# A convolution and a two-layer feed-forward block in one kernel: how the first layer's three passes are ordered and combined

## The chip, the core and the metric

The kernel runs on one core of a Trainium2 chip. Each time is the device time of one execution in microseconds; three runs of the kernel before are given and their median is the figure that counts. The profile comes from one profiled execution. TensorE (PE; its weight loads are listed as PEld), VectorE (DVE), ScalarE (ACT), GpSimd (POOL) and SyncE (SP, which here only starts DMA transfers) each have an instruction queue of their own and wait for one another by semaphores.

## The reference

The input `x` has 8 sequences of 4096 tokens with 192 channels. A causal convolution with seven taps, whose weights are a softmax over the taps of each head, gives 32,768 tokens of 192 channels. Then two dense layers with a gate between them:

```python
w = softmax(weight)                     # per head, over the 7 taps
y = causal_conv(x, w)                   # (32768, 192)
h = y @ w_in                            # (32768, 2048)
g = h * np.clip(h + 3.0, 0.0, 6.0) / 6.0
out = g @ w_out                         # (32768, 192), float32
```

## The kernel before, in words

**Blocks.** The tokens are worked off in 32 blocks of 1024. Block 0 is run by a start section of its own, while the weights are being loaded and converted; blocks 1 to 31 are each one call of `first_layer` followed by one call of `second_layer`. A block's 1024 tokens stand as two groups of 512: partitions 0 to 63 of the tile `y` hold the lower 512 tokens, partitions 64 to 127 the upper 512, and the 192 channels are three thirds of 64. A 64-row matmul uses half of TensorE's array, so a matmul on the lower half (`k` = 0) and one on the upper half (`k` = 1) can run side by side; they write two different PSUM banks. `y_other` holds the same parts with the two halves exchanged (each exchange is two DMA transfers on SyncE, lines 266 and 267), so that each chunk of `w_in` meets each token group.

**First layer.** `h = y @ w_in` is done per unit: a unit is one chunk of 128 hidden columns, from one half of the hidden columns on the lower array half and from the other on the upper one, for 512 tokens each. There are 16 units per block, 8 with `y_own` and 8 with `y_other`. A unit owns a slot, that is two PSUM banks out of eight; there are four slots, handed out in turn from `free_slots`. To keep nearly full float32 precision with TensorE's shorter number format (`fp32r` in the profile), each operand is split into a high part and a rest, and each unit makes three passes of six matmuls (three thirds, two array halves), line 516. In the kernel before, the three operands are HIGH, LOW and MIX, and the sum is built in two steps: after the passes HIGH and LOW the slot's two banks are multiplied in place by 4097 on ScalarE (line 528; for the last unit of a block ScalarE and VectorE take one bank each, lines 531 and 532), and the pass MIX is added on top. To give ScalarE the time, `first_layer` works two units ahead: `begin(n)` issues a unit's passes HIGH and LOW and the scaling, `end(n)` the pass MIX, and TensorE's order is begin 0, begin 1, end 0, begin 2, end 1, and so on; near the end begin 15 is issued ahead of end 13. `end(n)` then computes the gate: ScalarE's relu from PSUM into the tile `g` (`relu`, line 302) and VectorE's product with `h` from PSUM (`gate`, line 306), after which the slot may be used again.

At the first unit of each block one more matmul is issued first (line 508): lower half, one third, 256 columns, with the same operands as the full matmul that later overwrites its output. Within a pair, the upper half (`k` = 1) is issued first.

**Second layer.** `out = g @ w_out` is done with full float32 matmuls, 32 output columns each, four side by side (line 623), by a scheme that saves multiplications with sums of quarter matrices (`g_sums`, `small_sums`: lines 412, 456, 586 on VectorE and GpSimd). Its order is written out by hand as events with a due time: four streams of matmuls, and jobs `do(t, ...)` sorted in among them. The list `between` puts work for the next block there: `split_high` at 13, `split_rest` at 15, `swap_parts` at 18 (the parts of `y` and their exchange), and the load and first taps of the convolution for the block after next. The convolution's remaining taps (line 929, VectorE) are jobs in the first layer: one ahead of the units (`jobs[-1]`, together with what is left of the block before: two additions, their transposes and stores), and one each behind units 1, 5 and 9.

**The start.** `out_direct(0, ...)` is block 0's second layer (line 341). Between its matmuls `prepare` makes the parts of `w_in` (`w_parts`, in two halves of 1536 elements a partition: lines 474, 477, 485), convolves block 1, starts a load of `x` through GpSimd's queue and splits `y`; then `begin_block_two` makes sums of `w_out` and, on GpSimd, eight differences (line 595).

Each engine works through its instructions in the order in which the program issues them; nothing reorders them later.

Of the kernel before, what the change touches and what calls it, by code (L numbers as in the profile page):

```python
# [8 lines left out]
ALU = mybir.AluOpType  # L9
ACT = mybir.ActivationFunctionType  # L10
AX = mybir.AxisListType
F32 = mybir.dt.float32
# [5 lines left out]


CUT = 1.0 - 2.0**-13  # L20
EPS = 2.0**-12
HIGH, LOW, MIX = range(3)


@with_exitstack
def kernel(
# [8 lines left out]
    nc = tc.nc  # L35
    P = nc.NUM_PARTITIONS
# [6 lines left out]
    N = 512  # L43
    G = 2
    TB = G * N
    D2 = P // 2
    K3 = D // D2
# [7 lines left out]
    NP = NC // 2  # L55
# [32 lines left out]
    for base, dma in ((0, nc.scalar), (D2, nc.sync)):  # L88
        dma.dma_start(  # L89
            out=w_sb[base : base + D2],  # L90
            in_=weight.unsqueeze(1).to_broadcast([H, GJ, KC]),
# [126 lines left out]
    for n in range(AHEAD):  # L218
# [8 lines left out]
        out=e_sb[:], in0=w_sb[:], in1=mx[:].to_broadcast([P, KC]), op=ALU.subtract  # L227
# [4 lines left out]
    half = cst.tile([P, 1], F32, name="half")  # L232
# [4 lines left out]
    y = ys.tile([P, K3, N], F32, name="y")  # L237
# [27 lines left out]
    def swap(to, part):  # L265
        nc.sync.dma_start(out=to[D2:P], in_=part[0:D2])
        nc.sync.dma_start(out=to[0:D2], in_=part[D2:P])
# [10 lines left out]
    psum = ps.tile([P, 2 * 4, N], F32, name="psum")  # L278
# [22 lines left out]
    def relu(r6, h):  # L301
        nc.scalar.activation(r6, h, ACT.Relu, bias=half[:], scale=1.0 / 6.0)  # L302

    def gate(g_, h):

        nc.vector.scalar_tensor_tensor(  # L306
            out=g_, in0=g_, scalar=1.0, in1=h, op0=ALU.min, op1=ALU.mult
        )
# [93 lines left out]
    def g_sums(engine, which, slots, width):  # L402

        forms = {
            3: (S3, A11, A21, ALU.subtract),
            2: (S2, S1, A11, ALU.subtract), 4: (S3, A12, S2, ALU.subtract),
        }
        for n in which:
            o, a, b, op = forms[n]
            for p in slots[::width]:  # L410
                r = slice(p, p + width)
                engine.tensor_tensor(out=o[:, r], in0=a[:, r], in1=b[:, r], op=op)  # L412
# [42 lines left out]
    def add(out, x, y, op=ALU.add):  # L455
        nc.vector.tensor_tensor(out=out, in0=x, in1=y, op=op)  # L456
# [13 lines left out]
    def r32(ap):  # L470
        return ap.bitcast(F32R)

    def high_of(out, x, scale=1.0):
        nc.scalar.mul(r32(out), x, CUT * scale)

    def from_high(out, high, scale, x, op):
        nc.vector.scalar_tensor_tensor(
            out=r32(out), in0=high, scalar=scale, in1=x, op0=ALU.mult, op1=op
        )

    def w_parts(high, low, mix, w):
        high_of(high, w, EPS)
        from_high(mix, high, 4097.0, w, ALU.subtract)
        from_high(low, high, -4096.0, w, ALU.add)
        nc.scalar.mul(r32(mix), mix, -4096.0)

    free_slots = list(range(4))
    y_own, y_other, pools, s1 = [], [None], [], []

    def swap_parts():  # L490
        y_other[0] = pools[0].tile([P, 3, K3, N], F32, name="y_other", tag="other")
        for n in range(3):
            swap(y_other[0][:, n], y_own[n])


    def first_layer(i, jobs):

        slots = {}

        def both(n):  # L500
            return psum[:, 2 * slots[n] : 2 * slots[n] + 2]

        def mms(n, part, start=False, stop=False):
            group, c = divmod(n, NP)
            if n == 0 and start:

                r, half = slice(0, D2), slice(0, N // 2)
                nc.tensor.matmul(  # L508
                    out=psum[:, 2 * slots[n], half], lhsT=r32(w_in_parts[part][r, c, 0]),
                    rhs=r32(y_own[part][r, 0, half]), start=True, stop=False,  # L510
                    skip_group_check=True,
                )
            for s in range(K3):
                for k in (1, 0):
                    r = slice(k * D2, (k + 1) * D2)
                    nc.tensor.matmul(  # L516
                        out=psum[:, 2 * slots[n] + k], lhsT=r32(w_in_parts[part][r, c, s]),
                        rhs=r32(y_other[0][r, part, s] if group else y_own[part][r, s]),
                        start=start and s == 0, stop=stop and s == K3 - 1,
                        skip_group_check=True,  # L520
                    )

        def begin(n):
            slots[n] = free_slots.pop(0)
            mms(n, HIGH, start=True)
            mms(n, LOW)
            if n + 1 < count:
                nc.scalar.mul(both(n), both(n), 4097.0)  # L528
            else:
                lower, upper = (psum[:, 2 * slots[n] + k] for k in range(2))  # L530
                nc.scalar.mul(lower, lower, 4097.0)
                nc.vector.tensor_scalar(
                    out=upper, in0=upper, scalar1=4097.0, scalar2=None, op0=ALU.mult
                )

        def end(n):
            group, c = divmod(n, NP)
            mms(n, MIX, stop=True)
            to = g4[:, c, 1:3] if group else g4[:, c, 0::3]
            relu(to, both(n))  # L540
            gate(to, both(n))
            free_slots.append(slots[n])

        count = 2 * NP
        begin(0)
        begin(1)
        for job in jobs.get(-1, ()):
            job()
        for n in range(count):
            if n == count - 3:  # L550
                begin(n + 2)
            end(n)
            if n < count - 3:
                begin(n + 2)
            for job in jobs.get(n, ()):
                job()
            if n == 1:
                s1.append(ot.tile([P, NP, N], F32, name="s1", tag="shared")[:])
            if n < NP and n % 2:
                small_sums(s1[-1], A11, (1, 2, 3, 4), nc.gpsimd, every[n - 1 : n + 1])  # L560
            if n > NP and n % 2:
                pair = slice(n - NP - 1, n - NP + 1)
                g_sums(nc.gpsimd if n + 1 < count else nc.vector, (3,), range(NP)[pair], 2)
                if n + 3 < count:
                    nc.gpsimd.dma_start(out=S1[:, pair], in_=A22[:, pair], accum_op=ALU.add)
        for pair in (slice(NP - 2, NP), slice(NP - 4, NP - 2)):
            add(S1[:, pair], A21[:, pair], A22[:, pair])
# [7 lines left out]
    def small_sums(to, x, which, engine=nc.gpsimd, r=every):  # L575

        r = slice(r[0], r[-1] + 1)
        x11, x12, x21, x22 = four_parts(x[:, r])
        s1, s2, s3, s4 = four_parts(to[:, r])
        forms = {  # L580
            1: (s1, x21, x22, ALU.add), 2: (s2, s1, x11, ALU.subtract),
            3: (s3, x11, x21, ALU.subtract), 4: (s4, x12, s2, ALU.subtract),
        }
        for n in which:
            o, p, q, op = forms[n]
            engine.tensor_tensor(out=o, in0=p, in1=q, op=op)  # L586
# [222 lines left out]
    with tc.manual_schedule():  # L809
# [4 lines left out]
            out=c_sb[:], in0=e_sb[:], in1=sm[:].to_broadcast([P, KC]), op=ALU.mult  # L814
# [15 lines left out]
        for _ in range(3):  # L830

            nc.tensor.matmul(
                out=psum[:, b], lhsT=zeros[:, 0:P], rhs=zeros[:], start=True, stop=True
# [57 lines left out]
        slots = [0, 1, 3, 4, 6, 7, 9, 10, 12, 13]  # L891
        n = 3
# [30 lines left out]
        w_in_parts = [late.tile([P, NP, K3, P], F32, name=f"w_in{n}") for n in range(3)]  # L923
# [9 lines left out]
            return jobs  # L933

        def split_y():
            high, low, mix = y_own
            high_of(high[:], y[:])
            split_rest()

        def split_high():  # L940
            high_of(y_own[HIGH][:], y[:])

        def split_rest():
            high, low, mix = y_own
            nc.vector.tensor_tensor(out=r32(low[:]), in0=y[:], in1=high[:], op=ALU.subtract)
            from_high(mix[:], high[:], 1.0 + EPS, y[:], ALU.subtract)

        def prepare():
            for n in range(0, NP, 4):
                r = slice(n, n + 4)  # L950
                w_parts(*[w[:, r] for w in w_in_parts], w_in[:, r])
            for job in conv_jobs(1):
                job()
            first_in.close()
            later = ctx.enter_context(tc.tile_pool(name="later", bufs=1, reuse_waits="tile"))
            y_own.extend(later.tile([P, K3, N], F32, name=f"y{n}") for n in range(3))
            pools.append(ctx.enter_context(tc.tile_pool(name="oth", bufs=1, reuse_waits="tile")))
            x_tiles[2] = load_x(2, nc.gpsimd)
            split_y()
# [3 lines left out]
        def begin_block_two():  # L963
# [4 lines left out]
            for job in conv[:3]:  # L968
                job()

        out_direct(0, [prepare, lambda: None, begin_block_two])
        swap_parts()
        w_sums(((T3, B22, B12),))
# [53 lines left out]
```

## Time and profile before

| quantity | value |
|---|---|
| median of three runs | 2230.28 us |
| the three runs | 2229.96, 2230.28, 2230.80 us |
| profiled execution: span, first to last instruction | 2228.3 us |
| instructions | 50401 |
| granted TensorE clock, mean | 1.000 |
| busy PE / PEld | 2221.0 us (100%) / 1560.8 us (70%) |
| busy DVE / ACT / POOL | 1894.3 us (85%) / 1379.2 us (62%) / 823.6 us (37%) |
| matmuls of the first layer (L516), blocks 1 to 31 | 8928 |
| matmuls L508 | 31, 381 ns each |
| weight loads L516, mean | 184 ns |

For the profiled execution the records hold the span and no time of its own; the span lies 2.0 us under the median of the runs.

How to read it: "L516 PE MATMUL psum<-y,w_in 64*128 64x512" is a group of matmuls of line 516 that use 64 rows and 128 columns of the array and stream 512 columns; behind it stand the count, the busy time, the mean duration of one in ns, and the idle time of the engine just before them with what ended it. The durations of matmuls are modelled and overlap each other, so the rate of TensorE is read from starts, not from durations. The chain goes back from the last instruction, each time to what released it. TILE<-TILE names what is written and read: `psum<-psum` is an operation that works on PSUM in place. In a timeline's row stand the start, the time to the group's last end, the engine, the line, the operation and the count.

### The profile page before, as it was taken

What the parts mean: (1) busy time and instruction counts of PE and PEld (TensorE: products, weight loads), DVE (VectorE), ACT (ScalarE), POOL (GpSimd) and SP (SyncE); (2) the same over time, 40 slices, a digit from 0 to 9 for tenths busy, and PEclk for the clock granted to TensorE, in tenths of its full rate; (3) what the DMA queues carried; (4) which work ended last, traced back from release to release, by engine and by line L of the source; (5) the groups of instructions that cost most, each with busy time, mean ns of one, the idle gap of its engine ahead of it and who ended that gap; (6) DMA issues with size and microseconds to landing.
All of it is one profiled execution on the core that took longest, in us unless ns stands there. A gap on an engine that the chain in (4) does not pass through costs nothing.

```text
span 2228.3 us, 50401 instructions
## 1 busy us (share of the span) xinstructions
PE 2221.0 (100%) x21527; PEld 1560.8 (70%) x21527; DVE 1894.3 (85%) x1673; ACT 1379.2 (62%) x1678; POOL 823.6 (37%) x690
## 2 busy tenths in 40 slices
PE   9999999999999999999999999999999999999999
PEld 5477776677766777766777667786677776677766
DVE  8888888888888888888888888888888888888876
ACT  7457665576655676555766557665567655576654
POOL 2344432344422444223443234442244422344323
PEclk9999999999999999999999999999999999999999
DMA  6244224443244342344422443324434234442232
GB/s 157 58 98 84 49 58 91 85 83 63 53 82 91 77 80 46 71 91 84 84 48 58 91 87 81 67 49 82 91 78 82 47 67 91 84 84 52 55 77 34
DMA packets 253584, 166.58 MB, mean 75 GB/s; under 512 B 208016, under 2 KB 213136, under 8 KB 253360
## 3 DMA queue, kind: packets, MB, share of 16 engines
q1 hardware_dynamic: 234872, 129.46, 28.4%
q0 software_dynamic: 17248, 33.64, 8.7%
q8 instruction: 169, 2.77, 0.5%
q10 hardware_dynamic: 1240, 0.27, 0.1%
q14 instruction: 55, 0.45, 0.1%
HBM read 31.72 MB, written 25.17 MB: 26 GB/s over the span
## 4 chain that ended last, share of the span: by engine, by line
PE 99%; DMA 0%; DVE 0%; SPq 0%; ACT 0%; issue 0%; DVEq 0%; ACTq 0%
PE psum L623 49%; PE psum L516 46%; PE psum L296 2%; PE psum L341 2%; PE psum L508 0%; DMA x<-in_x_dram 0%; SPq L100 0%; SPq L133 0%; DVE top L175 0%; PE psum L824 0%; DVE y L255 0%; DVE results L456 0%; SPq L89 0%; ACT y L838 0%; ACT scale L186 0%
## 5 line engine op out<-in xcount | busy, mean ns | idle before, releaser
L623 PE MATMUL psum<-g,w_out 128*32 128x512 f32 (+1 forms) x6712 | 967.5, 552 | 0.0
L306 DVE SCALAR_TENSOR_TENSOR g<-g,psum 128x1024 f32<-128x1024 f32 (+1 forms) x528 | 618.3, 1186 | 203.6 <-ACT g L302 203.1
L586 POOL TENSOR_TENSOR s<-g 128x256 f32<-128x256 f32 x248 | 273.9, 1104 | 1244.4 <-DVE g L306 1244.4
L302 ACT ACTIVATE g<-psum,half 128x1024 f32<-128x1024 f32 (+1 forms) x528 | 564.8, 1086 | 4.9 <-PE psum L516 0.3
L623 PEld LDWEIGHTS psum<-g,w_out 128*32 128x32 f32 x6712 | 371.7, 110 | 246.0 <-issue 126.7
L516 PE MATMUL psum<-y,w_in 64*128 64x512 f32 x4464 | 524.9, 388 | 0.0
L516 PE MATMUL psum<-y_other,w_in 64*128 64x512 f32 x4464 | 516.1, 386 | 0.0
L528 ACT ACTIVATE psum<-psum 128x1024 f32<-128x1024 f32 x465 | 469.0, 1009 | 54.4 <-PE psum L516 52.1
L516 PEld LDWEIGHTS psum<-y,w_in 64*128 64x128 f32 x4464 | 435.4, 184 | 71.2 <-ACT psum L528 0.3
L516 PEld LDWEIGHTS psum<-y_other,w_in 64*128 64x128 f32 x4464 | 423.8, 184 | 82.1
L623 PE MATMUL psum<-s,w_out 128*32 128x512 f32 (+1 forms) x3272 | 465.5, 570 | 0.0
L929 DVE SCALAR_TENSOR_TENSOR y<-x,c_sb,y 128x1536 f32<-128x1536 f32 x186 | 335.3, 1803 | 2.6 <-ACT y L927 1.4
L412 POOL TENSOR_TENSOR s<-g 128x1024 f32<-128x1024 f32 x93 | 285.8, 3073 | 26.7 <-DVE g L306 26.5
L623 PE MATMUL psum<-g,w_s 128*32 128x256 f32 x1240 | 282.8, 379 | 0.0
L623 PEld LDWEIGHTS psum<-s,w_out 128*32 128x32 f32 x3272 | 154.3, 110 | 81.8 <-issue 49.4
L623 PEld LDWEIGHTS psum<-g,w_s 128*32 128x32 f32 x1240 | 136.4, 110 | 67.7
L412 DVE TENSOR_TENSOR s<-g 128x2048 f32<-128x2048 f32 (+1 forms) x93 | 181.3, 1977 | 1.1
L623 PE MATMUL psum<-s,w_s 128*32 128x256 f32 x744 | 170.7, 379 | 0.0
L586 DVE TENSOR_TENSOR g<-g 128x1024 f32<-128x1024 f32 x124 | 151.7, 1224 | 5.2
L412 DVE TENSOR_TENSOR g<-g 128x2048 f32<-128x2048 f32 x62 | 139.0, 2284 | 0.0
L620 ACT COPY psum<-psum 32x512 f32<-32x512 f32 x93 | 51.3, 551 | 135.4 <-PE psum L623 135.4
L456 DVE TENSOR_TENSOR results<-psum,results 32x256 f32<-32x256 f32 (+3 forms) x128 | 69.3, 541 | 50.9 <-issue 45.5
(93 smaller groups left out, 1316.6 us busy)
## 6 DMA issues: line engine op xcount, KB each, us to landing
y_other<-y SPq DMA_DIRECT2D x186, 384.0 KB, 5.1
g<-g POOLq DMA_DIRECT2D x62, 512.0 KB, 5.0
out_dram<-results SPq DMA_DIRECT2D x378, 64.0 KB, 2.0
x<-in_x_dram SPq DMA_DIRECT2D x53, 388.5 KB, 7.7
stage<-in_moe_w_in_dram SPq DMA_DIRECT2D x16, 192.0 KB, 4.8
stage<-in_moe_w_out_dram SPq DMA_DIRECT2D x8, 384.0 KB, 5.5
x<-in_x_dram SPq DMA_DIRECT2D x7, 384.0 KB, 8.3
x<-in_x_dram POOLq DMA_DIRECT2D x2, 388.5 KB, 5.3
```

What stands on the lines that cost most here:

```text
L296: nc.tensor.matmul(out=psum[:, b], lhsT=w[r], rhs=src, start=start, stop=stop, skip_group_check=onto,)
L302: nc.scalar.activation(r6, h, ACT.Relu, bias=half[:], scale=1.0 / 6.0)
L306: nc.vector.scalar_tensor_tensor(out=g_, in0=g_, scalar=1.0, in1=h, op0=ALU.min, op1=ALU.mult)
L341: lambda p=p: nc.tensor.matmul(out=bank[j * QS : (j + 1) * QS, tokens], lhsT=w_out[:, p, w, cols], rhs=x[:, p, tokens], start=(first and p ...
L412: engine.tensor_tensor(out=o[:, r], in0=a[:, r], in1=b[:, r], op=op)
L456: nc.vector.tensor_tensor(out=out, in0=x, in1=y, op=op)
L516: nc.tensor.matmul(out=psum[:, 2 * slots[n] + k], lhsT=r32(w_in_parts[part][r, c, s]), rhs=r32(y_other[0][r, part, s] if group else y_own[ ...
L528: nc.scalar.mul(both(n), both(n), 4097.0)
L586: engine.tensor_tensor(out=o, in0=p, in1=q, op=op)
L620: streams[3].append((t - 0.5, lambda: fn(*args, **kw)))
L623: nc.tensor.matmul(out=out, lhsT=w, rhs=x, start=start, stop=True, tile_position=(0, j * QS), skip_group_check=True,)
L929: jobs.append(lambda k=k: nc.vector.scalar_tensor_tensor(out=y[:], in0=x[:, :, k : k + N], scalar=c_sb[:, k : k + 1], in1=y[:], op0=ALU.mu ...
```

## The change

The three passes of a unit are now issued one after the other into the same slot, unit after unit, and add straight up: `w` HIGH with `y` HIGH, `w` LOW with `y` HIGH, `w` FULL with `y` LOW. The split is high = x times (1 - 2^-13) rounded to the short format, low = x - high. With `w = full`, this is w times low plus (high + low) times high. The in-place multiplication by 4097 goes, and with it `begin`, `end` and the two units of lead. `y` has two parts and not three, so two exchanges per block and not three. `w` keeps three parts: its LOW is now one subtraction on GpSimd, and FULL a copy on ScalarE. The extra matmul at the start of a block goes, and within a pair the lower half (`k` = 0) is issued first. The jobs of `jobs[-1]` are issued ahead of unit 0 (before: behind `begin(1)`, and thus ahead of unit 0's gate on VectorE too).

```diff
-HIGH, LOW, MIX = range(3)
+HIGH, LOW, FULL = range(3)
+PASSES = (HIGH, HIGH), (LOW, HIGH), (FULL, LOW)
...
-    def w_parts(high, low, mix, w):
-        high_of(high, w, EPS)
-        from_high(mix, high, 4097.0, w, ALU.subtract)
-        from_high(low, high, -4096.0, w, ALU.add)
-        nc.scalar.mul(r32(mix), mix, -4096.0)
+    def low_of(out, x, high, engine):
+        engine.tensor_tensor(out=r32(out), in0=x, in1=high, op=ALU.subtract)
+
+    def w_parts(high, low, full, w):
+        high_of(high, w)
+        nc.scalar.copy(out=r32(full), in_=w)
+        low_of(low, w, high, nc.gpsimd)
...
-        y_other[0] = pools[0].tile([P, 3, K3, N], F32, name="y_other", tag="other")
-        for n in range(3):
+        y_other[0] = pools[0].tile([P, 2, K3, N], F32, name="y_other", tag="other")
+        for n in range(2):
             swap(y_other[0][:, n], y_own[n])
...
-            if n == 0 and start:
-
-                r, half = slice(0, D2), slice(0, N // 2)
-                nc.tensor.matmul(
-                    out=psum[:, 2 * slots[n], half], lhsT=r32(w_in_parts[part][r, c, 0]),
-                    rhs=r32(y_own[part][r, 0, half]), start=True, stop=False,
-                    skip_group_check=True,
-                )
-            for s in range(K3):
-                for k in (1, 0):
...
-        def begin(n):
-            slots[n] = free_slots.pop(0)
-            mms(n, HIGH, start=True)
-            mms(n, LOW)
-            if n + 1 < count:
-                nc.scalar.mul(both(n), both(n), 4097.0)
...
-        def end(n):
-            group, c = divmod(n, NP)
-            mms(n, MIX, stop=True)
...
+        def unit(n):
             group, c = divmod(n, NP)
+            slot = free_slots.pop(0)
+            for m_, (wn, yn) in enumerate(PASSES):
+                for s in range(K3):
+                    for k in range(2):
+                        r = slice(k * D2, (k + 1) * D2)
+                        nc.tensor.matmul(
+                            out=psum[:, 2 * slot + k], lhsT=r32(w_in_parts[wn][r, c, s]),
+                            rhs=r32(y_other[0][r, yn, s] if group else y_own[yn][r, s]),
+                            start=m_ == s == 0, stop=m_ == 2 and s == K3 - 1,
+                            skip_group_check=True,
+                        )
+            both = psum[:, 2 * slot : 2 * slot + 2]
             to = g4[:, c, 1:3] if group else g4[:, c, 0::3]
-            relu(to, both(n))
-            gate(to, both(n))
-            free_slots.append(slots[n])
+            relu(to, both)
+            gate(to, both)
+            free_slots.append(slot)
...
         def split_rest():
-            high, low, mix = y_own
-            nc.vector.tensor_tensor(out=r32(low[:]), in0=y[:], in1=high[:], op=ALU.subtract)
-            from_high(mix[:], high[:], 1.0 + EPS, y[:], ALU.subtract)
+            low_of(y_own[LOW][:], y[:], y_own[HIGH][:], nc.vector)
```

More of the change, by code (lines that the diff above doesn't have):

```diff
@@ L20 @@
 CUT = 1.0 - 2.0**-13
-EPS = 2.0**-12
-HIGH, LOW, MIX = range(3)
+HIGH, LOW, FULL = range(3)
+PASSES = (HIGH, HIGH), (LOW, HIGH), (FULL, LOW)
 @with_exitstack
@@ L471, in r32, with high_of @@
         return ap.bitcast(F32R)
[L473 to L478, printed above, removed]
-        )
-    def w_parts(high, low, mix, w):
-        high_of(high, w, EPS)
-        from_high(mix, high, 4097.0, w, ALU.subtract)
-        from_high(low, high, -4096.0, w, ALU.add)
-        nc.scalar.mul(r32(mix), mix, -4096.0)
+    def high_of(out, x):
+        nc.scalar.mul(r32(out), x, CUT)
+    def low_of(out, x, high, engine):
[4 more added lines that the diff above has]
+        low_of(low, w, high, nc.gpsimd)
     free_slots = list(range(4))
@@ L490, in swap_parts @@
     def swap_parts():
-        y_other[0] = pools[0].tile([P, 3, K3, N], F32, name="y_other", tag="other")
-        for n in range(3):
+        y_other[0] = pools[0].tile([P, 2, K3, N], F32, name="y_other", tag="other")
+        for n in range(2):
             swap(y_other[0][:, n], y_own[n])
     def first_layer(i, jobs):
[L498 to L503, printed above, removed]
+        def unit(n):
@@ L504, in mms @@
             group, c = divmod(n, NP)
-            if n == 0 and start:
-                r, half = slice(0, D2), slice(0, N // 2)
-                nc.tensor.matmul(
-                    out=psum[:, 2 * slots[n], half], lhsT=r32(w_in_parts[part][r, c, 0]),
-                    rhs=r32(y_own[part][r, 0, half]), start=True, stop=False,
-                    skip_group_check=True,
-                )
-            for s in range(K3):
-                for k in (1, 0):
[L515 to L521, printed above, removed]
@@ L523, in begin @@
-        def begin(n):
-            slots[n] = free_slots.pop(0)
-            mms(n, HIGH, start=True)
-            mms(n, LOW)
-            if n + 1 < count:
[L528 to L534, printed above, removed]
@@ L539, in end @@
+            both = psum[:, 2 * slot : 2 * slot + 2]
             to = g4[:, c, 1:3] if group else g4[:, c, 0::3]
-            relu(to, both(n))
-            gate(to, both(n))
-            free_slots.append(slots[n])
+            relu(to, both)
+            gate(to, both)
+            free_slots.append(slot)
         count = 2 * NP
-        begin(0)
-        begin(1)
         for job in jobs.get(-1, ()):
@@ L549, in first_layer @@
         for n in range(count):
[L550 to L554, printed above, removed]
+            unit(n)
             for job in jobs.get(n, ()):
@@ L935, in split_y @@
         def split_y():
-            high, low, mix = y_own
-            high_of(high[:], y[:])
+            split_high()
             split_rest()
@@ L943, in split_rest @@
         def split_rest():
-            high, low, mix = y_own
-            nc.vector.tensor_tensor(out=r32(low[:]), in0=y[:], in1=high[:], op=ALU.subtract)
-            from_high(mix[:], high[:], 1.0 + EPS, y[:], ALU.subtract)
+            low_of(y_own[LOW][:], y[:], y_own[HIGH][:], nc.vector)
         def prepare():
@@ L955, in prepare @@
             later = ctx.enter_context(tc.tile_pool(name="later", bufs=1, reuse_waits="tile"))
-            y_own.extend(later.tile([P, K3, N], F32, name=f"y{n}") for n in range(3))
+            y_own.extend(later.tile([P, K3, N], F32, name=f"y{n}") for n in range(2))
             pools.append(ctx.enter_context(tc.tile_pool(name="oth", bufs=1, reuse_waits="tile")))
```

## The prediction

> **What bounds the kernel now.** I read the engine totals of the page first, then the chain that ended last, then one block of 1024 tokens (a repeating period) by stage, and last the starts of single matmuls.
>
> The page, sections 4 and 5:
>
> ```profile
> PE 99%; DMA 0%; DVE 0%; SPq 0%; ACT 0%; issue 0%; DVEq 0%; ACTq 0%
> L516 PE MATMUL psum<-y,w_in 64*128 64x512 f32 x4464 | 524.9, 388 | 0.0
> L528 ACT ACTIVATE psum<-psum 128x1024 f32<-128x1024 f32 x465 | 469.0, 1009 | 54.4 <-PE psum L516 52.1
> ```
>
> TensorE carries 99% of the chain, and its matmuls have 0.0 us of idle time. The scaled middle step (L528) is 469 us of ScalarE, and nothing of ScalarE is on the chain. So what counts is what the change does to TensorE's own succession. The chain of waits, cut to one block (start, us, what):
>
> ```profile
> 201.32 35.47 PE psum L623 x216
> 236.79 0.31 PE psum L508
> 237.10 8.00 PE psum L516 x69
> ```
>
> and engine busy time in that block's first layer (168.24 to 201.25) and second layer:
>
> ```profile
> 168.24:201.25 33.01, 33.01 (x290) 27.40 (x289) 25.85 (x23) 30.74 (x32) 21.95 (x19) 1.00 0.15 25
> 201.25:236.72 35.47, 35.47 (x386) 21.15 (x384) 32.76 (x28) 11.90 (x20) 3.59 (x2) 1.00 0.59 119
> ```
>
> Columns: stretch, us, then busy us (instructions) of PE, PEld, DVE, ACT, POOL, then clock, DMA share, GB/s. The reader is to see a period of 68.48 us, run 31 times, TensorE without a gap in either half at a clock of 1.00, and ScalarE at 30.74 of 33.01 us in the first half: nearly full, yet TensorE doesn't wait for it. In the waits of the weight loader, ScalarE's L528 stands with 0.3 us in two waits.
>
> How fast does TensorE step? A first-layer matmul has 64 rows; the lower (k=0) and the upper half (k=1) of the array work side by side, in pairs, 144 pairs a block. Matmul timelines, each of a narrow window (so the first start in it is read):
>
> ```profile
> 168.24 0.38 PE L508 MATMUL psum<-y,w_in 64*128 64x256 f32 x1
> 168.24 0.49 PE L516 MATMUL psum<-y,w_in 64*128 64x512 f32 x1
> 168.46 3.16 PE L516 MATMUL psum<-y,w_in 64*128 64x512 f32 x25
> 171.00 0.62 PE L516 MATMUL psum<-y,w_in 64*128 64x512 f32 x3
> 171.91 0.40 PE L516 MATMUL psum<-y,w_in 64*128 64x512 f32 x2
> 200.71 0.39 PE L516 MATMUL psum<-y_other,w_in 64*128 64x512 f32 x2
> ```
>
> L508 starts together with the upper half's first matmul, takes the lower half for 256 columns, and so puts the lower half half a step behind. From 168.46 to 171.00 lie 25 - 3 = 22 starts, 11 steps of 2.54/11 = **0.231 us**. Near 171.1 the two halves fall into step (two matmuls now start at 171.91 as one), and from pair 16 (171.91) to pair 143 (200.71) lie 127 steps of 28.80/127 = **0.2268 us**. The weight loader shows the same two states: in 168.45 to 171.05 it is busy 2.51 of 2.60 us (the two halves load in turn), in 171.65 to 200.90 it is 24.18 of 29.25 (both load at once).
>
> **The change, part by part.**
>
> *L508 goes, the order within a pair turns from (1, 0) to (0, 1).* Today pair 143 starts 200.71 - 168.24 = 32.47 us after the stage's first matmul. Without L508 I expect both halves to start at 168.24 in step. The first matmul shows its weight load: 0.49 us against the mean of 0.39, so the second pair comes 0.227 + 0.10 = 0.33 us later; the first-layer matmuls of the start, which have no such extra matmul, do just this (pairs at 17.12, 17.65 and 18.08, thus 0.53 and then 0.43). Then 141 steps of 0.2268 us = 31.98. Pair 143 starts after 32.31 us: **0.16 us less per block, 31 x 0.16 = 5.0 us**. It comes from two places: the lower half begins its first full matmul 0.22 us sooner, and 11 steps of 0.231 become 0.2268 (0.05 us); against them stands that the relock at 171.1 today costs the upper half, which ran ahead, and not the pair. Bounds of this unknown: were the halves to stay out of step all stage, 0.33 + 141 x 0.231 = 32.90, a loss of 0.43 us per block (13 us); were all of L508's piece in the chain to go, a gain of 0.31 us (9.6 us). I take 0.16, as 127 of 143 steps in every block already show the rate. The gap ahead of the stage (167.71 to 168.24) and the one behind it (200.94 to 201.25) stay.
>
> *Three passes in a row instead of 12 matmuls of two units ahead.* The number of L516 matmuls stays at 18 per unit, 8,928 in all, of the same shapes. In the order of TensorE a unit's sum is complete after 18(n+1) matmuls instead of 18n + 30; only the last three units (today at 276, 282, 288 of 288) change by more: 252, 270, 288. Every relu and gate (L302, L306) is thus ready as early as today or up to 24 matmuls sooner, so nothing in the second layer gets later.
>
> *The scaled middle step goes (L528, L531, L532).* Per block 15 x 1.01 + 0.58 = 15.7 us of ScalarE and 0.70 us of VectorE. All of it lies beside TensorE: worth nothing. What is late next is nothing on the path, as TensorE has no idle.
>
> *The waits that remain.* A unit's first matmul waits for the gate that frees its PSUM slot, four units before. Queued behind it is all of TensorE. Now the tile jobs of the block before (two adds, two transposes, one convolution tap) stand ahead of the first gate on VectorE, as they do today: they end at 171.63 + 1.77 = 173.4. Then gate 0 to 174.6, gate 1 to 175.8, a tap of 1.8 to 177.6, gate 2 to 178.8. Unit 4 begins at 168.24 + 0.33 + 35 x 0.2268 = 176.5, unit 6 at 180.6: the cover is 1.8 to 1.9 us (today unit 4 begins at about 175.9 and gate 0 ends at 174.9: 1.0). Units 1 to 3 take banks that the second layer leaves last; their waits come later than today (at matmul 18, 36, 54 instead of 12, 30, 48), and today they cost nothing. If one were late, it would cost at least one shown weight load, 0.10 us per block, 3.1 us.
>
> *The third operand goes.* Per block 1.76 us of VectorE (L477), and two of six y_other transfers of SyncE (384 KB, 5.1 us to landing), all during the second layer: hidden, worth nothing.
>
> *The weights' parts, once, during 58 to 100 us.* VectorE loses four operations of 1.91 us; ScalarE keeps four; GpSimd gets two subtractions of 128x1536. Its row for 128x1024 is 3.07 us, so an estimate of 4.6 us each. GpSimd's last join ends at 67.0, so they end near 76; the second pass that needs them begins at 100.5 (99.72 + 0.33 + two steps). Behind them on GpSimd stand the load of x for block 2, which today waits until 88.06 for VectorE, and the eight w_s differences from 89.37: unmoved. Cover 24 us; beyond it each us costs one.
>
> Sum: 2228.3 - 5.0 = 2223.3 us of span. The median of the three runs stands 2.0 us above the profiled span (2230.28 against 2228.3), and I carry that over: **2225.3 us**.
>
> **Where the Trainium skill speaks against this.** The row: 127 steps in step at 0.2268 us, weight loads hidden. The Trainium skill (TensorE: Matmul & The Clock Gate, Part 3, on what overlaps) says that a weight load runs beside matmuls in flight only where its row group is another one. By that rule it is the staggered start that hides loads, and removing L508 would expose one per pair. The rows speak against it: while in step, both halves load during their own matmuls.
>
> **Rivals.**
>
> 1. *The gain is eaten* (14%): one or two waits at the new unit borders end after TensorE arrives, 0.10 us each per block, one leaves 0.06 of the 0.16, two lose 0.04. Time 2228.4 or 2231.5. For it: each of the first three units waits now for ScalarE or VectorE; against it: those waits come 0.7 us later than today.
> 2. *Out of step* (9%), the slower side: without L508 the halves start 4 ns apart and drift into alternation as they do in 168.46 to 171.00, at 0.231 us. Price 0.43 us per block: 2243. It decides if the alternation holds past pair 40 or so: at 0.004 us a step, 40 steps eat the gain. Against it: after 171.1 nothing drifts.
> 3. *VectorE late for the slots* (3%): slower once VectorE runs over 1.8 us behind in a block; 1 us beyond costs 31 us: 2256. Against it: it idles before single gates already today.
> 4. *Loads exposed in step* (1%): 0.10 us for each of 142 steps, 31 times, 440 us: 2670. Against it are the 127 steps.
> 5. *All of the chain's piece goes* (6%): 0.31 us per block, 2220.7. For it: the chain shows it as a piece of its own; against it: the first matmul must then show its load instead.
> 6. *ScalarE paces the first layer* (1%), as its 98% in 171.65 to 200.90 would suggest: steps would fall toward the 0.215 of the second layer's half-width matmuls (L623 128x256, in the timeline two of them start 0.43 us after two others), 0.012 x 143 x 31 = 53 us, 2177. Against it: no idle on PE.
>
> **How the numbers follow.** Forecast 66%, with 0.13 to 0.19 us per block: 2224.4 to 2226.3. The runs of before spread by 0.8 us, so its own range is 2224.2 to 2226.6. Forecast and rival 1 hold 80%: the range is 2224.2 to 2231.5, and leaves out rivals 2 to 6. A measurement of this kernel can tell about 0.2% from no change, 4.5 us, that is 0.144 us per block; most of the forecast (54 of 66) lies beyond it. Faster: 54 + 6 + 1 = 61%. Same: 12 + 14 = 26%. Slower: 9 + 3 + 1 = 13%.
>
> **What would show it right or wrong.** After the change a block's period should be 68.33 us; the stage's two first matmuls should both last 0.49 and start together; the weight loader should stand near 83% from the stage's first microsecond; ScalarE should fall by 487 us to some 892, VectorE by 84 us to some 1810, with PE still 99% of the chain. It is wrong if the stage's early steps are 0.231 (rival 2), if a unit border shows a matmul of 0.49 us again (rival 1), or if PE's load waits name DVE or ACT in the first layer (rival 3).

## The result, and the profile after

| | before | after |
|---|---|---|
| median of 14 runs each | 2230.24 us | 2225.70 us |
| ratio, 95% interval | | 0.998 [0.9972, 0.9988] |
| profiled span | 2228.3 us | 2223.6 us |
| a block's period (first matmul of one first layer to that of the next, median of the blocks) | 68.487 us | 68.340 us |
| busy PEld / DVE / ACT / POOL | 1560.8 / 1894.3 / 1379.2 / 823.6 us | 1536.0 / 1810.3 / 938.1 / 819.8 us |
| moved by DMA | 166.58 MB | 142.10 MB |

The kernel is 4.5 us faster; 2225.3 us was forecast. The period accounts for the gain: 31 x (68.487 - 68.340) = 4.56 us. Lines after the change are numbered anew: the first layer's matmuls are L508 (before L516), the second layer's L593 (before L623), relu L308, gate L312.

The page of after, sections 4 and 5:

```profile
PE 99%; DMA 0%; DVE 0%; SPq 0%; ACT 0%; issue 0%; DVEq 0%; ACTq 0%
L308 ACT ACTIVATE g<-psum,half 128x1024 f32<-128x1024 f32 (+1 forms) x528 | 574.2, 1092 | 487.8 <-PE psum L508 459.8
L508 PE MATMUL psum<-y,w_in 64*128 64x512 f32 x4464 | 515.3, 388 | 0.0
```

TensorE still makes the whole chain, and its matmuls still have no idle time. ScalarE, freed of the scaling, now waits 459.8 us for TensorE in front of the relu: its time has turned into idle time, not into a shorter kernel. The same block as before in the chain of waits:

```profile
194.98 6.12 PE psum L508 x54
201.10 35.47 PE psum L593 x216
236.57 8.62 PE psum L508 x73
```

The second layer's piece is 35.47 us as before. The piece of L508's old extra matmul is gone; the first-layer stage is what got shorter. Engine busy time by stage (columns as before):

```profile
168.16:201.03 32.87, 32.87 (x289) 26.90 (x288) 26.91 (x23) 17.35 (x16) 23.50 (x21) 1.00 0.18 29
201.03:236.50 35.47, 35.47 (x386) 21.15 (x384) 29.26 (x26) 11.07 (x19) 2.07 (x1) 1.00 0.46 94
```

The first half is 32.87 us against 33.01; ScalarE in it 17.35 against 30.74. Now the matmul starts after the change, each from a narrow window, so that a row's first start is read:

```profile
168.16 0.50 PE L508 MATMUL psum<-y,w_in 64*128 64x512 f32 x2
168.50 0.39 PE L508 MATMUL psum<-y,w_in 64*128 64x512 f32 x2
169.89 0.39 PE L508 MATMUL psum<-y,w_in 64*128 64x512 f32 x2
171.02 0.62 PE L508 MATMUL psum<-y,w_in 64*128 64x512 f32 x4
171.93 0.39 PE L508 MATMUL psum<-y,w_in 64*128 64x512 f32 x2
200.49 0.39 PE L508 MATMUL psum<-y_other,w_in 64*128 64x512 f32 x2
```

These are pairs 1, 2, 8, 13, 17 and 143. Both halves start as one, both first matmuls last 0.50 us (a weight load shown), the second pair comes 0.34 us later. Pair 143 starts 32.33 us after the stage's first matmul; before it was 32.47. From pair 17 on there are 126 steps in 28.56 us, 0.2267 each. From pair 2 to pair 13, though, 11 steps take 2.52 us, 0.229 each: the slow early steps are there after the change too. It is the first six of them that are slow (to pair 8, 1.39 us, 0.232 each); the five behind them take 1.13 us, 0.226 each. And the weight loader, stretch by stretch:

```profile
168.45:171.05 2.60, 2.10 (x26) 1.00 0.00 0
171.65:200.90 29.25, 23.99 (x258) 1.00 0.19 31
```

At 81% and 82% it shows the two halves in step from the first microseconds; before, the first stretch had 2.51 of 2.60.

### The profile page after: what moved, and what is told of

Its sections match the earlier page's. It is cut to its first block, busy times and chain, and to the rows that moved or that the text cites. A ratio compares the mean times of both kernels' runs of the same rounds, so it can differ in the third digit from the quotient of the medians.

```text
span 2223.6 us, 49133 instructions
## 1 busy us (share of the span) xinstructions
PE 2216.4 (100%) x21496; PEld 1536.0 (69%) x21496; DVE 1810.3 (81%) x1607; ACT 938.1 (42%) x1182; POOL 819.8 (37%) x692
## 2 busy tenths in 40 slices
DMA packets 248613, 142.10 MB, mean 64 GB/s; under 512 B 207024, under 2 KB 212144, under 8 KB 248400
## 4 chain that ended last, share of the span: by engine, by line
PE 99%; DMA 0%; DVE 0%; SPq 0%; ACT 0%; issue 0%; DVEq 0%; ACTq 0%
PE psum L593 49%; PE psum L508 46%; PE psum L302 2%; PE psum L347 2%; DMA x<-in_x_dram 0%; SPq L106 0%; SPq L139 0%; DVE top L181 0%; PE psum L794 0%; DVE y L261 0%; DVE results L462 0%; SPq L95 0%; ACT y L808 0%; ACT scale L192 0%; ACT sig L195 0%
## 5 line engine op out<-in xcount | busy, mean ns | idle before, releaser
L593 PE MATMUL psum<-g,w_out 128*32 128x512 f32 (+1 forms) x6712 | 967.4, 552 | 0.0
L308 ACT ACTIVATE g<-psum,half 128x1024 f32<-128x1024 f32 (+1 forms) x528 | 574.2, 1092 | 487.8 <-PE psum L508 459.8
L312 DVE SCALAR_TENSOR_TENSOR g<-g,psum 128x1024 f32<-128x1024 f32 (+1 forms) x528 | 619.6, 1185 | 195.5 <-ACT g L308 195.1
L556 POOL TENSOR_TENSOR s<-g 128x256 f32<-128x256 f32 x248 | 267.0, 1077 | 1252.9 <-DVE g L312 877.3
L593 PEld LDWEIGHTS psum<-g,w_out 128*32 128x32 f32 x6712 | 371.8, 110 | 246.3 <-issue 126.9
L508 PE MATMUL psum<-y,w_in 64*128 64x512 f32 x4464 | 515.3, 388 | 0.0
L508 PE MATMUL psum<-y_other,w_in 64*128 64x512 f32 x4464 | 510.9, 386 | 0.0
L508 PEld LDWEIGHTS psum<-y,w_in 64*128 64x128 f32 x4464 | 415.8, 184 | 112.3 <-issue 26.0
L508 PEld LDWEIGHTS psum<-y_other,w_in 64*128 64x128 f32 x4464 | 418.1, 184 | 87.8
L593 PE MATMUL psum<-s,w_out 128*32 128x512 f32 (+1 forms) x3272 | 465.4, 570 | 0.0
L418 POOL TENSOR_TENSOR s<-g 128x1024 f32<-128x1024 f32 x93 | 297.8, 3203 | 25.0 <-DVE g L312 25.0
L593 PE MATMUL psum<-g,w_s 128*32 128x256 f32 x1240 | 282.8, 379 | 0.0
L593 PEld LDWEIGHTS psum<-s,w_out 128*32 128x32 f32 x3272 | 154.5, 110 | 80.2 <-issue 48.3
L593 PEld LDWEIGHTS psum<-g,w_s 128*32 128x32 f32 x1240 | 136.4, 110 | 67.7
L593 PE MATMUL psum<-s,w_s 128*32 128x256 f32 x744 | 170.7, 379 | 0.0
L462 DVE TENSOR_TENSOR p<-psum,p 32x256 f32<-32x256 f32 (+1 forms) x93 | 47.7, 513 | 95.5 <-PE psum L593 94.1
```

The costliest lines, as they stand in the source:

```text
L312: nc.vector.scalar_tensor_tensor(out=g_, in0=g_, scalar=1.0, in1=h, op0=ALU.min, op1=ALU.mult)
L508: nc.tensor.matmul(out=psum[:, 2 * slot + k], lhsT=r32(w_in_parts[wn][r, c, s]), rhs=r32(y_other[0][r, yn, s] if group else y_own[yn][r, s ...
L593: nc.tensor.matmul(out=out, lhsT=w, rhs=x, start=start, stop=True, tile_position=(0, j * QS), skip_group_check=True,)
```

## The experiments

Two explanations were set against each other. **S**: what counts is how the stage starts and whether the two halves are held up; the work of the other engines is worth nothing. **L** and the other rivals: the extra matmul's own time, or the time of ScalarE, VectorE or the transfers. Periods are medians over the blocks of each kernel's trace. Each run stands beside the median of the kernel before that was timed along with it (2230.35 or 2230.25 us); "period above after" compares the periods of two traces.

### The extra matmul alone taken out

```diff
-            if n == 0 and start:
-                ... # the 256-column matmul of line 508
```

> The kernel before without the extra half-width matmul (L508), all else as before: one part of the change alone. Theory S (the gain is the start in step, and it needs the unbroken passes too): the two halves start in step, and twelve pairs (two units' HIGH and LOW) end at 168.24 + 0.33 + 11 x 0.2275 = 171.08 in block 2. But the sum of unit 0's first two passes is now ready about 0.1 us later (its sixth pair starts near 169.73, before at 169.62), so the scaling on ScalarE ends near 171.17 and the third pass begins near 171.2 with its weight load shown in both halves; pair 14 comes near 171.56, before at 171.45. So about 0.1 us more per block: 2233 us, the range 2230 to 2235. Rival L (the gain is L508's own time): 2225.7, as after the change.

Measured: 2226.81 us against 2230.35, ratio 0.9984 [0.9975, 0.9993]; period 68.374 us. The number of S was wrong, and nearly that of L came out: one part of the change alone brings 0.113 of the 0.147 us per block. S had counted the sixth pair one step too late. The waits of the weight loader show what the scaling did in fact:

```profile
PEld psum L508 <- ACT psum L520: 5.0, 31, 0.2
```

(here L508 is the first-layer matmul and L520 the scaling). Once per block the loads of pair 13 wait 0.16 us for the scaling, which ends at 170.90 in block 2. The loads begin at 170.95 and the pair starts on time at 171.05, so no load is shown. But the eight steps behind it take 1.84 us, 0.230 each, like those behind a stage's start, and this is 0.03 us: the 68.374 - 68.340 = 0.034 by which this kernel's period stays above that of after.

The kernel before has the same wait, though its view of waits names it only twice (0.3 us). In block 2 the scaling and the loads of TensorE beside it are:

```profile
170.05 1.01 ACT L528 ACTIVATE psum<-psum 128x1024 f32<-128x1024 f32 x1 [1.13 <-PE psum L516]
170.78 0.18 PEld L516 LDWEIGHTS psum<-y,w_in 64*128 64x128 f32 x1
171.11 0.54 PEld L516 LDWEIGHTS psum<-y,w_in 64*128 64x128 f32 x6
```

The loader stands from 170.96 to 171.11, until just behind the scaling's end at 171.06. By the trace it stands like this in all 31 blocks: 0.162 us in the two that the view names, 0.149 to 0.150 us in the other 29.

### The extra matmul put back into the kernel after

```diff
+            if n == 0:
+                nc.tensor.matmul(out=psum[:, 2 * slot, 0:256], lhsT=<lower half, HIGH>,
+                    rhs=<lower half, HIGH, 256 columns>, start=True, stop=False, ...)
...
-                    for k in range(2):
+                    for k in (1, 0):
```

> The kernel after, with the extra matmul of 256 columns put back at each block's start, and the upper half first in a pair, as before. Theory S: the lower half is half a step behind, and as no wait for a scaling brings the halves into step again, all 143 steps are 0.231 us: pair 143 starts 0.22 + 142 x 0.231 = 33.0 us after the stage's start, after the change 32.33: 0.68 us per block, 21 us, 2247 us. The weight loader stands near 97% through the whole first layer. Rival L (L508 costs its own time, about 0.15 us): 2230.3.

Measured: 2229.61 us against 2230.35, ratio 0.9996 [0.9987, 1.0005]; period 68.466 us, 0.126 above after. S was right that the halves then stay half a step apart through the whole stage, as the weight loader shows, busy nearly without a pause:

```profile
171.65:200.90 29.25, 29.13 (x257) 1.00 0.18 31
```

It was wrong in what that costs: 2247 us was S's number, and L's 2230.3 was near. Two starts of the lower half in this state, 126 steps apart (L515 is the first layer's matmul here):

```profile
171.80 0.61 PE L515 MATMUL psum<-y,w_in 64*128 64x512 f32 x3
200.36 0.72 PE L515 MATMUL psum<-y_other,w_in 64*128 64x512 f32 x4
```

28.56/126 = 0.2267 us: out of step is exactly as fast as in step. The 0.231 us of the prediction belongs to a stage's first steps, in either state: the first six behind pair 2 when the halves are in step, nine here. What the extra matmul costs is paid at the start: 0.126 us.

### Twice the columns

```diff
-            256 columns
+            512 columns (a whole step; the rest as in the run above)
```

> As the run with the extra half-width matmul, but the extra matmul streams 512 columns: twice the extra work, but a whole step, so that the halves stay in step. Theory S: one step of 0.227 us per block, 7.0 us, 2232.7 us, thus less than with half the work. Rival L: twice the cost of the half-width one: 2235 if that costs 4.6 us, 2268 if that costs 21.

Measured: 2232.94 us against 2230.35, ratio 1.0012 [1.0003, 1.0021]; period 68.573 us, 0.233 above after. One whole step, as S had it (2232.7). S had expected the smaller matmul to cost more than this one, which fell with the run above; L's proportion (0.126 for 256 columns, 0.233 for 512) remains possible here, and the run with 32 columns below decides on it.

### The scaling alone taken out

```diff
-            if n + 1 < count:
-                nc.scalar.mul(both(n), both(n), 4097.0)
-            else:
-                ... # lines 531 and 532
```

> The kernel before without the scaling of the partial sums (lines 528, 531, 532), with its extra matmul and its order of two units ahead; the factor 4097 is left out of the result. Theory S: work is taken away, yet it gets slower: nothing holds the third pass up near 171.1, the halves stay half a step apart to the end of the stage, 130 more steps of 0.231 in place of 0.2268 us, 0.5 us per block: 2245 to 2248 us. Rival (ScalarE's 15.7 us per block cost time): faster than 2230.2. Rival (the halves come into step by themselves within some microseconds): 2230.2.

Measured: 2229.48 us against 2230.35, ratio 0.9996 [0.9987, 1.0005]; period 68.466 us. Taking 15.7 us of ScalarE per block out of the kernel before moves its period by 0.021 us. The halves stay out of step to the end (weight loader 29.25 of 29.25 us in 171.65 to 200.90), so it is indeed the wait for the scaling that puts them in step in the kernel before; but S's price for it (2245 to 2248 us) was wrong again, for the reason above. The time is near the second rival's 2230.2, though not by its mechanism, as the halves don't come into step. The period is that of the run with the extra matmul in the kernel after: the order of the passes and the third operand make no difference.

### What the other engines were spared, put back

```diff
+            nc.scalar.mul(spare[:], w_full[:, 0 : 2 * N], 4097.0)   # per unit
             relu(to, both)
...
-        for n in range(2):
-            swap(y_other[0][:, n], y_own[n])
+        for n in range(3):
+            swap(y_other[0][:, n], y_own[min(n, LOW)])
...
             low_of(y_own[LOW][:], y[:], y_own[HIGH][:], nc.vector)
+            low_of(y_own[LOW][:], y[:], y_own[HIGH][:], nc.vector)
```

> The kernel after, with what the change took off the other engines put back as idle work: per unit a 128x1024 ScalarE multiplication (about 1.0 us) ahead of the relu, per block a second 128x1536 subtraction on VectorE (1.75 us) and a third pair of exchanges on SyncE. Theory S: all of it lies beside TensorE: 2225.7 us, a block's period 68.34 us. Rival (the time of ScalarE, VectorE or the transfers counted): part of the way back to 2230.2.

Measured: 2226.03 us against 2230.25, ratio 0.9981 [0.9972, 0.999]; period 68.340 us, to the nanosecond that of after. The first-layer stage of block 2:

```profile
168.16:201.03 32.87, 32.87 (x292) 26.90 (x288) 26.79 (x23) 31.91 (x32) 23.42 (x21) 1.00 0.18 29
```

ScalarE is at 31.91 of 32.87 us, more than in the kernel before, and TensorE's stage is as long as without. Not put back are VectorE's share of the scaling (0.70 us per block) and its work on the weights in the start. S holds; the time of these engines was not on the path.

### The order within a pair

```diff
-                    for k in range(2):
+                    for k in (1, 0):
```

> The kernel after, with the upper half first in each pair, as before. Theory S: 2225.7 us, period 68.34 us; the order within a pair is worth nothing. Rival (the order is part of the gain): up to 2230.

Measured: 2225.66 us against 2230.25, ratio 0.998 [0.9971, 0.9989]; period 68.340 us. The order is worth nothing.

### Neither extra matmul nor scaling, in the kernel before

```diff
-            if n == 0 and start:
-                ... # line 508
...
-            if n + 1 < count:
-                ... # lines 528, 531, 532
```

> The kernel before without the extra matmul and without the scaling (lines 528, 531, 532; the factor 4097 is left out of the result), but with its order of two units ahead and its three parts: the fourth corner of a square of which before is 68.487 us a block, without the extra matmul 68.374, without the scaling 68.466. Theory S: without either 68.340, as after the change, thus 2225.7 us: the two causes are the extra matmul and one wait for the scaling, and the order of the passes is worth nothing. Rival (the unbroken passes have a gain of their own): 68.37 or more, 2226.7.

Measured: 2225.54 us against 2230.25, ratio 0.9979 [0.997, 0.9988]; period 68.340 us. This closes the square (us per block):

| | scaling waited for | no scaling |
|---|---|---|
| with the extra matmul | 68.487 (before) | 68.466 |
| without it | 68.374 | 68.340 (and after: 68.340) |

The two causes hold the whole gain per block. The extra matmul is 0.113 to 0.126 us, the one wait per block 0.021 to 0.034 us. The unbroken passes have no gain of their own beyond not needing that wait.

### An extra matmul of 32 columns

```diff
-            256 columns
+            32 columns (the rest as in the run with 256)
```

> The kernel after with the extra matmul at each block's start cut to 32 columns (upper half first, as in the run with 256, which took 68.466 us a block, 0.126 more than after). Theory S, sharpened: the extra matmul costs a weight load of its own in the lower half, 0.107 us, and not its columns: 256 columns stream just while the next load runs. So 32 columns cost the same: 68.45 to 68.47 us, 2229.2 to 2229.7. Rival (its columns cost): 32 of 512 columns are 0.014 us a block, 2226.2.

Measured: 2228.81 us against 2230.25, ratio 0.9994 [0.9984, 1.0003]; period 68.440 us, 0.100 above after.

```profile
168.30 0.28 PE L506 MATMUL psum<-y,w_in 64*128 64x32 f32 x1
168.30 0.49 PE L515 MATMUL psum<-y,w_in 64*128 64x512 f32 x1
```

L506 is the extra matmul. The first full matmuls of the two halves together, from the groups of the window 168.40 to 168.50:

```profile
L515 PE MATMUL psum<-y,w_in 64*128 64x512 f32 x2 | 0.6, 484 | 0.0
```

An eighth of the columns costs 0.100 us and not 0.014; 256 columns cost 0.126. It is a little under S's 68.45 to 68.47, but a price in proportion to the columns is ruled out. With 32 columns what is paid is a weight load that nothing covers: the upper half's first full matmul lasts 0.49 us, so of the mean of 0.484 the lower half's has 0.48 in place of 0.39; its load shows too, behind that of the extra matmul. With 256 columns the two parts can't be told apart, as the columns' own time (half a step, 0.113 us) is about as long as a load (0.1 us, from 0.50 against 0.39). With 512 columns the price, 0.233, is that of a whole step of columns. So S's "and not its columns" holds for the small one alone; that the longer of the two counts is a reading of these three prices.

## Why the prediction was right, and where not

**The bound** was right: TensorE alone sets the end, and a block's period is the sum of its own starts. That made the small extra matmul worth more than 441 us of ScalarE.

**The start in step** was right in its form: both halves start at once, the load is shown once (0.34 us to the second pair, worked out as 0.33 from a first matmul of 0.49 us against 0.39), and behind the first steps 0.2267 us a step follow. The size was 0.16 us per block; measured are 0.147. It is the difference of two stage lengths, 32.47 us read from the trace and 32.31 built from measured steps, and the built one came out at 32.33; so the total did not hang on how the prediction shared the gain out, and that was partly wrong. The share that was mis-sized is "11 steps of 0.231 become 0.2268 (0.05 us)". They became 0.229, worth 0.02. The runs show why: the 0.231 is not the price of being out of step, but of the first steps behind a start or a wait of the loader. In step and out of step both end at 0.2267. What remains is the delay of the lower half by the extra matmul (0.126 us by the run that puts it back) and the wait (0.021).

**That the relock "today costs the upper half, which ran ahead, and not the pair"** was nearly right: by the run without the scaling it costs the block 0.021 us.

**"All of it lies beside TensorE: worth nothing"**, of the scaling, was right for its busy time (put back: the same period) and wrong for its wait. The prediction read 0.3 us in two waits of the weight loader; the trace has one of 0.15 us in each of the 31 blocks, and the slower steps behind it are what it costs. That alone is 0.7 to 1.1 us of the 4.5.

**The remaining waits, the third operand, the weights' parts**: all at nothing, as priced. GpSimd's two subtractions of the weights took 6.9 us together, against an estimate of 4.6 each, and ended at 74.0. A relu now waits for GpSimd, 28.1 us in all, and VectorE has its gates 195 us of idle behind ScalarE; no TensorE load waits for either in the first layer: in the trace of after, its loader stands idle for over 0.06 us only ahead of a stage's first load. ScalarE fell by 441 us and not by the 487 of the sum of its rows: in the kernel before, scaling and relu overlapped by about 0.1 us each time in the records, so the rows' sum exceeds the engine's busy time.

**Rivals.** The first (a wait at a unit's border) doesn't show: of the 8,928 first-layer matmuls only the first pair of each of the 31 stages lasts 0.50 us, all others under 0.40. Nor need a wait cost the 0.10 us at which it was priced: the one in the run without the extra matmul costs 0.034. The second (out of step, 13 us) had a true premise, as the halves can stay apart for a whole stage, and a wrong price: the run that did it is 3.9 us over after. The third (VectorE late) doesn't show in the loads either. The fifth (all of the chain's 0.31 us piece) fell, as the first full matmul now shows its load. The sixth (ScalarE paces) falls with the run that puts ScalarE's work back. The fourth was that loads are exposed in step. The Trainium skill (TensorE: Matmul & The Clock Gate, Part 3, on what overlaps) says that weight loads run beside matmuls in flight only where the row group is another one. The traces say otherwise: 126 steps of 0.2267 us with both halves loading at once, the same as with the halves alternating. The loads that show after the change are a stage's first, 0.10 us.

The description of the kernel before says that nothing reorders an engine's instructions. For TensorE's weight loads the trace shows that this goes too far:

```profile
168.27 0.19 PEld L508 LDWEIGHTS psum<-y,w_in 64*128 64x128 f32 x2
```

These are the loads of the second pair after the change. The upper half's starts at 168.27, ahead of the lower half's matmul of that pair at 168.50, which the program issues before it.

What stays open is why the first steps behind a stage's start (six in step, nine out of step) and the eight behind the wait are about 2% slower, 0.231 against 0.2267 us; no run here tells what limits them.

## What to carry to other kernels

Where one engine has no idle time, price a change by that engine's own starts: an engine that is 98% busy beside it can be worth nothing, while one small instruction in its own stream costs a fraction of a microsecond each time. Look at what is exposed at the seams (the first weight load behind a switch, the loads behind a wait), for there a 32-column matmul costs nearly what a 256-column one does. A view of waits that names few of them can still leave out one in every block. And before giving a slow stretch to a state that goes with it, see whether the same stretch is slow in the other state too.

## What the runs showed of the hardware

- Two 64-row matmul streams side by side run at 0.2267 us per 512-column step whether they start together or half a step apart, and without a wait they keep whichever phase they were started in for a whole stage of 33 us; in the kernel before, the wait for the scaling put them in step.
- A wait of the weight loader that is over just in time (loads at 170.95, the pair on time at 171.05) still cost 0.03 us, in slower steps behind it.
- Behind a change from 32-column to 64-row matmuls the first weight load is not hidden: 0.50 us for a matmul that otherwise shows 0.39. An extra matmul placed there cost 0.100 us with 32 columns, 0.126 with 256 and 0.233 with 512.
